# Attention, top-1 experts and a gated network in one program: V copied on chip, a third q/k buffer, decay rows on another queue, expert unit 0 inside attention's last steps

## The chip, the cores and the metric

The program runs on one NeuronCore of one Trainium2 chip. The metric is the device time of one execution in microseconds; the kernel before has a median of 932.3 us over three runs (931.89 to 935.76).

## The reference

Three stages follow each other, all in float32 as the caller sees it.

```python
# 1. causal attention with a decay, batch 4, 8 heads, 576 positions, head size 64
scores = q @ k.T / 8 + cum[:, None] - cum[None, :]      # cum: running sum of log f
attn   = softmax(where(causal, scores, -1e9));  x = attn @ v
# 2. top-1 mixture of 8 experts over the 2304 tokens (x: 512 wide)
logits = x @ w_gate + modality_bias[modality_id];  e = argmax(logits)
x      = gate_w * (relu(x @ w1[e]) @ w2[e])             # w1: 512x1024, w2: 1024x512
# 3. gated network
out    = (sigmoid(x @ w_gate2) * (x @ w_val)) @ w_out   # 512 -> 1536 -> 512
```

## The kernel before

Attention works on 16 pairs: one head of two batches at a time (the second batch in reversed order, so that both halves fill the array). `Attention.run` is a software pipeline over n. In one step it takes the scores and exponentials of pair n, the transposes of q and k of pair n+1 (`prep`) and its decay mask (`mask`), the transposed probabilities and the product with V of pair n-1 (`probs`, `values`), and the division by the sums and the gate logits of pair n-2 (`normalise`, `logits`). The order of these pieces inside a step is written out by hand in `Attention.ORDER`: QA to QD are score products, T the additions of the mask with the running maximum, E the exponentials, PQ, PK, PR with pq, pk, prq, prk the transposes of q and k and their copies, X, Y, Z, W with their small letters the probabilities, A, AH, M the products with V, N1, N0, N2 the normalisation, D the mask, LQ, LV, LD the loads, L one piece of later work. Each engine receives its instructions in that order (manual schedule) and runs them in order.

Loads are issued by SyncE: q and k into raw buffers (`load_qk`), V into buffers `vr` (`load_v`) and two decay rows per pair, spread over all lanes (`load_dec`). The mask of pair 0 is made on VectorE, the others on GpSimd. V's pieces are loaded in two layouts, so some rows are read twice from memory.

When the first half of the tokens is done, small routing pieces (`Routing.early`) are taken from a list: they choose the first two blocks of tokens, units 0 and 1, while attention goes on, and fetch their rows. `Experts` splits each weight piece into a high and a low part for products of full precision. Unit 0's pieces are loaded and split by `begin`, after attention, into spare buffers of attention (decay masks and scores); its eight blocks of products (`pair`: up, relu, down) stand in the order behind attention. `Routing.finish` is the rest of the routing, a long chain on VectorE; its result is needed from unit 2 on, and unit 1 follows it in the order.

Of the kernel before, what the change touches and what calls it, by code (L numbers as in the profile page):

```python
# [84 lines left out]
class Attention:  # L85


    NV, NR = 3, 2
    ORDER = (
        "QA ot QB om PK T1 Y0 pk W w ra LQ Ta Z y0 X0 z Tb x0 LV N1 PQ T0 n1 E1 X1 x1 QC pq E4 QD PR prq T3 "  # L90
        "prk Y1 E3 N2 A0 D y1 M N0 AH E0 T2 n2 rc A3 A2 E2 LD A1 L L"
    )

    def __init__(self, tc, ctx, top, ro, ps, q, k, v, f):
# [11 lines left out]
        self.spares = 0  # L106
# [9 lines left out]
        nc.sync.dma_start(fs, f.rearrange("b h s -> (b h) s"))  # L116
        self.load_qk(0)
        V = nc.vector
# [7 lines left out]
        nc.sync.dma_start(self.drow[0], cum)  # L126
        nc.sync.dma_start(
# [10 lines left out]
    def spare(self, tag, shape, dt):  # L138

        if tag == "s":  # L140
            self.spares += 1
            pool, tag = ((self.ps_, "sc"), (self.pd, "dec"))[(self.spares - 1) // 2 % 2 == 0]
        else:
            pool, tag = {"e": (self.pe, "raw"), "t": (self.pt, "qk")}[tag]
        return pool.tile(shape, dt, tag=tag, name="e" + tag)
# [19 lines left out]
    def load_v(self, n):  # L165
# [241 lines left out]
    def run(self):  # L407
# [3 lines left out]
        while n < N + 2 or late:  # L411
            step = {"L": lambda: late.pop(0)() if late else None}
            if n == 2:
                self.ro.biases()
            if n == 4:
                self.ro.tables()
            if 0 <= n + 1 < N:
                step |= {"LV": lambda: self.load_v(n + 1), "D": lambda: self.mask(n + 1)}
                step |= self.prep(n + 1)
            if n + 2 < N:  # L420
                step |= {"LQ": lambda: n + 2 and self.load_qk(n + 2), "LD": lambda: self.load_dec(n + 2)}
            if 0 <= n < N:
                step |= self.scores(n)
# [8 lines left out]
            for key in self.ORDER.split():  # L432
                if key in step:
                    step[key]()
            if n == 0:
                self.ro.load()
            if 2 <= n < N + 2 and n % 2:
                late += self.ro.columns(*self.pairs[n - 2])
            n += 1


class Routing:
# [43 lines left out]
    def load(self):  # L486
# [1150 lines left out]
```

## Time and profile before

| | us |
|---|---|
| median of three runs | 932.3 |
| profiled execution, whole | 931.75 |
| its span, first to last instruction | 929.7 |
| TensorE busy | 874.8 (94%) |
| VectorE busy | 687.7 (74%) |
| ScalarE busy | 530.3 (57%) |
| GpSimd busy | 219.3 (24%) |

By stage, attention takes from the start to about 235 us, unit 0 lies from 232 to 257, the other units end near 484, and the gated network fills the rest. An engine that is off the path may stand idle without cost; the rows below therefore show stretches and single waits, not only sums. In a timeline the bracket at a row's end is the idle time of that engine before the row, and what ended it.

### The profile page before, as it was taken

Reading aid. Unit: us, or ns where it says so; the run is one execution under the profiler, and the core shown is the slowest. Engines: PE = TensorE matmul, PEld = TensorE weight load, DVE = VectorE, ACT = ScalarE, POOL = GpSimd, SP = SyncE. Lnnn points to the kernel's source line nnn. Section 1 sums busy time; section 2 is a strip of 40 time slices with the busy share of each in tenths; the row PEclk is TensorE's granted clock in tenths of the full one; section 3 lists DMA queues with packets and bytes.
Section 4 is the critical chain, followed back from the end, with each engine's and each line's share of the span. In section 5 each row is a group of like instructions: output and inputs, shape, how many; then the busy total and the mean of one; then the engine's idle time right before and its main releaser. Section 6 shows DMA issues by size and latency. Waiting matters only on the chain. (4 is left out here: it accounts for less than half of the span.)

```text
span 929.7 us, 16504 instructions
## 1 busy us (share of the span) xinstructions
PE 874.8 (94%) x5535; PEld 763.3 (82%) x5535; DVE 687.7 (74%) x1676; ACT 530.3 (57%) x1139; POOL 219.3 (24%) x457
## 2 busy tenths in 40 slices
PE   5899999868989999999989989999999999999996
PEld 3677667646879999999879878899998999999995
DVE  6567668864878999999856786988656888666662
ACT  3467667634356666666855455556545556544442
POOL 2678767486032222211000000001100001100002
PEclk8799999988999999999999999999999999999998
DMA  6577867985573695558928442225312222322201
GB/s 149 107 169 161 128 148 183 127 216 123 115 255 117 217 322 186 172 179 268 308 74 296 128 139 95 72 69 169 104 65 68 68 69 87 118 69 68 68 1 68
DMA packets 128411, 128.87 MB, mean 139 GB/s; under 512 B 75264, under 2 KB 102400, under 8 KB 128320
## 3 DMA queue, kind: packets, MB, share of 16 engines
q1 hardware_dynamic: 123680, 113.05, 44.3%
q0 software_dynamic: 4640, 14.70, 4.6%
q8 instruction: 45, 0.74, 0.3%
q14 instruction: 46, 0.38, 0.1%
HBM read 129.13 MB, written 24.28 MB: 165 GB/s over the span
## 5 line engine op out<-in xcount | busy, mean ns | idle before, releaser
L1335 PE MATMUL g<-x,wc 128*128 128x384 f32 x1536 | 303.4, 339 | 9.6 <-ACT pc L1372 3.1
L1335 PEld LDWEIGHTS g<-x,wc 128*128 128x128 f32 x1536 | 275.0, 189 | 29.9 <-ACT pc L1372 4.4
L1423 PE MATMUL o<-wo,ah 128*128 128x512 f32 x648 | 184.5, 397 | 0.2 <-DVE ah L1360 0.2
L1423 PEld LDWEIGHTS o<-wo,ah 128*128 128x128 f32 x648 | 118.0, 188 | 11.6 <-DVE ah L1360 1.0
L1431 POOL DMA_INDIRECT out_dram<-os,tok x18 | 18.4, 1021 | 421.7 <-ACT os L1430 416.2
L934 DVE TENSOR_TENSOR wl<-ws,wh 128x1024 fp32r<-128x1024 f32 x80 | 97.1, 1216 | 0.0
L928 ACT ACTIVATE wh<-ws 128x1024 fp32r<-128x1024 f32 x80 | 84.6, 1059 | 18.6 <-PE y L1010 18.6
L1359 ACT ACTIVATE ah<-s 128x384 fp32r<-128x384 f32 x72 | 37.9, 526 | 99.5 <-DVE s L1358 96.1
L272 ACT ACTIVATE sc<-sc,mn 128x192 f32<-128x192 f32 (+2 forms) x144 | 82.4, 577 | 7.2 <-DVE mn L264 7.1
L197 POOL TENSOR_SCALAR dec<-cum 128x192 f32<-128x192 f32 (+4 forms) x150 | 78.8, 533 | 18.6 <-DMA cum<-drow 15.5
L264 DVE CUSTOM_DVE_ANT_0 sc<-s,dec 128x192 f32<-128x192 f32 (+2 forms) x144 | 58.8, 441 | 23.4 <-PE s L257 18.3
L1000 PE MATMUL h<-xh,wh 128*128 128x256 f32 x256 | 74.2, 290 | 0.0
L1000 PE MATMUL h<-xh,wl 128*128 128x256 f32 x256 | 73.0, 285 | 0.7 <-DVE wl L934 0.7
L1000 PE MATMUL h<-xl,wh 128*128 128x256 f32 x256 | 73.0, 285 | 0.6 <-DVE xl L955 0.6
L980 POOL DMA_INDIRECT rows_by_expert<-ys,dst x20 | 22.8, 1138 | 197.5 <-ACT hh L970 135.0
L1372 ACT ACTIVATE pc<-g 128x384 f32<-128x384 f32 x96 | 46.3, 482 | 31.1 <-PE g L1335 31.1
L1218 DVE TENSOR_TENSOR wc<-wf,wc 128x512 fp32r<-128x512 f32 x72 | 40.7, 568 | 29.1 <-ACT wc L1215 29.1
L257 PE MATMUL s<-qk,qT 64*128 64x320 f32 (+4 forms) x384 | 60.0, 439 | 1.4 <-ACT qT L221 0.7
L291 PE MATMUL t<-ident,sc 128*128 128x128 f32 x320 | 50.5, 293 | 9.2 <-ACT py L297 6.7
L257 PEld LDWEIGHTS s<-qk,qT 64*128 64x128 f32 (+1 forms) x384 | 33.8, 192 | 27.6 <-issue 20.1
L1000 PEld LDWEIGHTS h<-xl,wh 128*128 128x128 f32 x256 | 49.4, 193 | 2.3 <-DVE xl L955 0.8
L1351 ACT ACTIVATE sg<-sg 128x384 f32<-128x384 f32 x48 | 25.2, 525 | 45.3 <-DVE sg L1381 18.8
(281 smaller groups left out, 1765.1 us busy)
## 6 DMA issues: line engine op xcount, KB each, us to landing
ws<-in_moe_w_dram SPq DMA_DIRECT2D x80, 512.0 KB
wf<-wd SPq DMA_DIRECT2D x36, 512.0 KB
cum<-drow SPq DMA_DIRECT2D x32, 288.0 KB
wd<-dec SPq DMA_DIRECT2D x18, 512.0 KB
wof<-wd SPq DMA_DIRECT2D x18, 512.0 KB
raw<-in_moe_w_gate_dram SPq DMA_DIRECT2D x12, 512.0 KB
raw<-in_moe_w_val_dram SPq DMA_DIRECT2D x12, 512.0 KB
raw<-in_moe_w_out_dram SPq DMA_DIRECT2D x12, 512.0 KB
```

The lines of the kernel that those rows point to most:

```text
L197: (nc.gpsimd if n else nc.vector).tensor_scalar(d[r, o], c[r, z], -1.0, c[r, a:a + 1], ALU.mult, ALU.add)
L257: nc.tensor.matmul(out[r, o:o + w], q[a, rows], k[a, c:c + w], start=True, stop=True)
L264: nc.vector.tensor_tensor_reduce(s[:, so + c0:so + e], t[j, b, c0][:, 0:e - c0], d[:, do + c0:do + e], -1.0, mn[j][:, 5:6] if c0 else 3.0e ...
L272: nc.scalar.activation(so, so, AF.Exp, bias=mn[j][:, b:b + 1], scale=-1.0, accum_out=sm[:, c:c + 1])
L291: nc.tensor.transpose(dst, s[:, o:o + P], self.ident)
L928: self.nc.scalar.activation(hi, self.wraw(u, k), AF.Copy)
L934: ins = eng.tensor_tensor(lo, self.wraw(u, k), hi.bitcast(F32), ALU.subtract)
L1000: nc.tensor.matmul(t, a[:, c, cs], b[:, c, :], start=(n == 0), stop=(n == 3 * KD - 1))
L1218: V(t["w"][:, 1, to], of(), t["w"][:, 0, to].bitcast(F32), ALU.subtract)
L1335: self.nc.tensor.matmul(t, p[:, c, :], q[:, c, :], start=(first and n == 0), stop=(n == total - 1), skip_group_check=not first)
L1372: nc.scalar.activation(c, t, AF.Copy)
L1423: nc.tensor.matmul(o[0], x[:, cs], y[:, r, :], start=(o[1] == 0 and k == 0), stop=(o[1] == 2 * self.NP - 1 and k == 2))
```

## The change

The table `ORDER` is written anew, and a table `TAIL` is added for the two steps that only drain (steps 16 and 17). The number of V buffers goes from 3 to 2 and that of the raw q/k buffers from 2 to 3. q and k are loaded for pair n+3 in step n; V is loaded for pair n, at the head of step n. Of V the repeated chunks are not loaded again but copied on ScalarE (`copy_v`, VC in the table). f, the running sums and the first pair's decay rows are issued by ScalarE. The gate logits begin with a copy, and the modality bias is added at head 3.

Unit 0 is prepared inside attention: its rows are fetched in step 13, its first four weight pieces are loaded at the end of step 13 and the other four at the end of step 15, its x is transposed in step 14, and its blocks (U in the table) stand between the pieces of steps 16 and 17. Pieces 0 and 1 are split on GpSimd, 2 and 3 (P2, P3) on ScalarE and VectorE, the others as before. The conversion of the four destination indices moves from ScalarE to GpSimd.

```diff
-    NV, NR = 3, 2
+    NV, NR = 2, 3
...
+    TAIL = (
+        "om ot U N1 n1 P2 U N2 N0 n2 Y0 y0 X0 x0 Z z X1 x1 Y1 y1 ra W w P3 U A0 M A1 A2 AH A3 rc U",
+        "U ot om U N1 n1 N2 N0 n2 U",
+    )
...
-        nc.sync.dma_start(fs, f.rearrange("b h s -> (b h) s"))
+        nc.scalar.dma_start(fs, f.rearrange("b h s -> (b h) s"))
         self.load_qk(0)
+        self.load_qk(1)
...
-        nc.sync.dma_start(self.drow[0], cum)
-        nc.sync.dma_start(
+        nc.scalar.dma_start(self.drow[0], cum)
+        nc.scalar.dma_start(
...
-        nc.sync.dma_start(t[0:64, 0, 4:9], a[:, 0:9:2])
+        nc.sync.dma_start(t[0:64, 0, 8], a[:, 8])
+        nc.sync.dma_start(t[64:P, 1, 8], b[:, 8])
         nc.sync.dma_start(t[0:64, 1, 4], b[:, 0])
-        nc.sync.dma_start(t[64:P, 1, 5:9], b[:, 2:9:2])
+
+    def copy_v(self, n):
+
+        t = self.vr[n % self.NV]
+        self.nc.scalar.activation(t[0:64, 0, 4:8], t[0:64, 0, 0:4], AF.Copy)
+        self.nc.scalar.activation(t[64:P, 1, 5:8], t[64:P, 1, 1:4], AF.Copy)
...
-            nc.sync.dma_start(t, self.drow[j, r:r + 1, :].to_broadcast([P, S]))
+            (nc.sync if n else nc.scalar).dma_start(t, self.drow[j, r:r + 1, :].to_broadcast([P, S]))
...
+            if 2 <= n + 3 < N:
+                step["LQ"] = lambda: self.load_qk(n + 3)
             if 0 <= n < N:
+                step |= {"LV": lambda: self.load_v(n), "VC": lambda: self.copy_v(n)}
...
-        nc.gpsimd.tensor_tensor(self.lg[:, sl], t[:, 0:k], (self.lg if h else self.bt)[:, sl], ALU.add)
+        lg, t = self.lg[:, sl], t[:, 0:k]
+        if h == 0:
+            nc.gpsimd.tensor_copy(lg, t)
+        else:
+            nc.gpsimd.tensor_tensor(lg, t, lg, ALU.add)
+        if h == 3:
+            nc.gpsimd.tensor_tensor(lg, lg, self.bt[:, sl], ALU.add)
...
-            nc.scalar.activation(self.dst0, dst, AF.Copy)
+            g.tensor_copy(self.dst0, dst)
...
-    POOL0 = 0, 1, 2, 3
+    POOL0 = 0, 1
...
-    def begin(self, att):
+    def prepare0(self, att, part):
 
         self.att = att
-        for k in range(8):
-            self.raw[k] = att.spare("e", [P, 1024], F32)
-        for k in range(8):
+        if part == 0:
+            for k in range(8):
+                self.raw[k] = att.spare("e", [P, 1024], F32)
+        for k in range(4 * part, 4 * part + 4):
             self.load(0, k)
-        for p in range(4):
-            self.high(0, p)
-            self.low(0, p)
-        self.run0 = self.pair(0, self.step0)
-        for f in range(8):
+        if part:
+            for p in self.POOL0:
+                self.split0(p)
+            self.run0, self.n0 = self.pair(0, self.step0), 0
+
+    def split0(self, p):
+        self.high(0, p)
+        self.low(0, p)
+
+    def advance(self):
+        if self.n0 < 8:
+            self.n0 += 1
             next(self.run0)
+
+    def begin(self):
+        while self.n0 < 8:
+            self.advance()
...
-        ro.then = [lambda c=c: ex.transpose(0, c) for c in range(0, KD, 2)]
+        none = lambda: None
+        ro.then = [lambda: ex.prepare0(att, 0)] + [lambda c=c: ex.transpose(0, c) for c in range(0, KD, 2)]
+        ro.then += [none, none, lambda: ex.prepare0(att, 1)]
```

Line numbers shift: a score product is L257 before and L263 now, a unit's up-projection L1000 and L1039, its down-projection L1010 and L1049.

VectorE at the start, before: the copies of k (`qk<-t`), the mask of pair 0 (`dec<-cum`) and the first addition (`sc,mn<-s,dec`).

```order
L125 SCALAR_TENSOR_TENSOR x<-ones,x 32x576
L484 COPY iw<-ident 64x8x64 x2
L219 COPY qk<-t 128x512
L219 COPY qk<-t 128x64
L197 TENSOR_SCALAR dec<-cum 128x192 x2
L197 TENSOR_SCALAR dec<-cum 128x576 x2
L197 TENSOR_SCALAR dec<-cum 64x64 x2
L197 TENSOR_SCALAR dec<-cum 128x448 x2
L197 TENSOR_SCALAR dec<-cum 128x320 x2
L264 ISA sc,mn<-s,dec 128x192
```

The same place now:

```order
L129 SCALAR_TENSOR_TENSOR x<-ones,x 32x576
L501 COPY iw<-ident 64x8x64 x2
L225 COPY qk<-t 128x64
L203 TENSOR_SCALAR dec<-cum 128x192 x2
L203 TENSOR_SCALAR dec<-cum 128x576 x2
L203 TENSOR_SCALAR dec<-cum 64x64 x2
L203 TENSOR_SCALAR dec<-cum 128x448 x2
L203 TENSOR_SCALAR dec<-cum 128x320 x2
L225 COPY qk<-t 128x512
L270 ISA sc,mn<-s,dec 128x192
```

The large copy of k has moved from ahead of the mask to behind it.

GpSimd in step 15, before: splits of unit 0's pieces (`edec<-eraw`), the logits of the normalisation (`lg<-lt`), the destination indices (`dstf`) and the fetch of the rows (`xg`).

```order
L926 TENSOR_SCALAR edec<-eraw 128x1024
L558 TENSOR_TENSOR lg<-lt,lg 128x24
L693 TENSOR_SCALAR pad_3339<-slot,n_90 128x2
L934 TENSOR_TENSOR edec<-eraw,edec 128x1024
L696 TENSOR_TENSOR dstf<-pad_3339,slot 128x2
L693 TENSOR_SCALAR pad_3339<-slot,n_90 128x2
L695 TENSOR_SCALAR row_3340<-slot,n_90 128x2
L696 TENSOR_TENSOR dstf<-pad_3339,row_3340 128x2
L697 TENSOR_TENSOR nt<-n_90 128x1
L702 DMA xg_92<-xd,ids_75 128x513
```

GpSimd from step 15 to step 17 now (the split buffers are all named `spare`):

```order
L581 TENSOR_TENSOR lg<-lt,lg 128x48
L338 TENSOR_SCALAR r<-sm 128x9
L581 TENSOR_TENSOR lg<-lt,lg 128x24
L965 TENSOR_SCALAR spare<-spare 128x1024
L973 TENSOR_TENSOR spare<-spare 128x1024
L965 TENSOR_SCALAR spare<-spare 128x1024
L973 TENSOR_TENSOR spare<-spare 128x1024
L581 TENSOR_TENSOR lg<-lt,lg 128x48
L581 TENSOR_TENSOR lg<-lt,lg 128x24
L338 TENSOR_SCALAR r<-sm 128x9
```

The fetch and the indices have left this place for steps 13 and 14; the splits of pieces 0 and 1 stand behind the logits of step 15, ahead of those of step 16.

TensorE at the end of step 15, before: the products with V of pair 14 (`o<-py,vr`), unit 0's transposes (`x<-ident,xg`), then the probabilities of pair 15 (`t<-ident,sc`).

```order
L348 MATMUL o<-py_3358,vr_126 64x384
L348 MATMUL o<-py_3359,vr_126 64x384
L953 MATMUL x<-ident,xg_92 128x128 x2
L953 MATMUL x<-ident,xg_93 128x128 x2
L953 MATMUL x<-ident,xg_92 128x128 x2
L953 MATMUL x<-ident,xg_93 128x128 x2
L291 MATMUL t<-ident,sc 128x128 x4
```

TensorE at the end of step 15 now: unit 0's first block (`h<-xh,spare`) follows the products with V at once, and the normalisation (`t<-iw,ot`) comes behind it.

```order
L354 MATMUL o<-py_3431,vr_124 64x128
L354 MATMUL o<-py_3432,vr_124 64x128
L1039 MATMUL h<-xh_3394,spare 128x256
L1039 MATMUL h<-xl_3395,spare 128x256
L1039 MATMUL h<-xh_3394,spare 128x256 x2
L1039 MATMUL h<-xl_3395,spare 128x256
L1039 MATMUL h<-xh_3394,spare 128x256 x2
L1039 MATMUL h<-xl_3395,spare 128x256
L1039 MATMUL h<-xh_3394,spare 128x256 x2
L1039 MATMUL h<-xl_3395,spare 128x256
L1039 MATMUL h<-xh_3394,spare 128x256
L395 MATMUL t<-iw,ot 128x144 x3
```

Unit 0's eight blocks stood behind the last product with V; now seven of them lie between there and the last normalisation, and the eighth follows it.

## Rows read from the trace of the kernel before

**Rows 1.** Table of stretches: length, busy time (instructions), granted clock, DMA share, GB/s.

```profile
66.00:112.00 46.00, 46.00 (x436) 33.94 (x434) 32.96 (x132) 32.13 (x97) 36.38 (x113) 1.00 0.81 154
...
42.00:44.00 2.00, 2.00 (x11) 2.00 (x10) 0.69 (x1) 0.51 (x1) 0.00 (x0) 0.50 0.41 94
```

**Rows 2.** Timeline of TensorE, one undisturbed step: start, us, line, operation.

```profile
53.96 1.83 PE L257 MATMUL s<-qk,qT 64*128 64x256 f32 x16
55.72 0.66 PE L226 MATMUL t<-ident,kr 128*128 128x128 f32 x4
56.21 0.60 PE L291 MATMUL t<-ident,sc 128*128 128x128 f32 x4
...
58.09 0.92 PE L389 MATMUL t<-iw,ot 128*128 128x144 f32 x6
58.85 0.60 PE L226 MATMUL t<-ident,qr 128*128 128x128 f32 x4
...
62.36 1.08 PE L348 MATMUL o<-px,vr 128*64 128x512 f32 x4
...
65.37 1.83 PE L257 MATMUL s<-qk,qT 64*128 64x256 f32 x16
```

**Rows 3.** Timeline of TensorE at the head and in the transition.

```profile
10.31 3.24 PE L257 MATMUL s<-qk,qT 64*128 64x256 f32 x16 [0.38 <-ACT qT L221]
...
41.46 1.09 PE L226 MATMUL t<-ident,kr 128*128 128x128 f32 x4 [3.10 <-DMA kr<-in_k_dram]
...
198.89 1.83 PE L257 MATMUL s<-qk,qT 64*128 64x256 f32 x16
...
209.04 1.12 PE L291 MATMUL t<-ident,sc 128*128 128x128 f32 x4 [6.75 <-ACT py L297]
```

**Rows 4.** Waits of TensorE, 60 to 200 us: total, times, longest.

```profile
PE t L226 <- DMA kr<-in_k_dram: 5.9, 4, 3.1
```

**Rows 5.** Timeline of TensorE: a down and an up of unit 0; unit 1's start.

```profile
240.47 1.52 PE L1010 MATMUL y<-edec,eqk 128*128 128x512 f32 x6
241.83 0.28 PE L1000 MATMUL h<-xh,esc 128*128 128x256 f32 x1
...
260.51 0.39 PE L1000 MATMUL h<-xh,wl 128*128 128x256 f32 x1 [0.75 <-DVE wl L934]
```

**Rows 6.** Timelines of GpSimd and ScalarE in step 15.

```profile
202.49 1.04 POOL L926 TENSOR_SCALAR edec<-eraw 128x1024 fp32r<-128x1024 f32 x1
...
204.22 2.34 POOL L934 TENSOR_TENSOR edec<-eraw,edec 128x1024 fp32r<-128x1024 f32 x1
...
207.81 0.20 ACT L698 ACTIVATE dst<-dstf 128x4 int32<-128x4 f32 x1 [8.63 <-POOL dstf L696]
```

**Rows 7.** Timeline of VectorE at the start.

```profile
8.69 0.69 DVE L219 COPY qk<-t 128x512 f32<-128x512 f32 x1 [1.98 <-PE t L226]
...
12.66 3.21 DVE L197 TENSOR_SCALAR dec<-cum 128x192 f32<-128x192 f32 x9 [0.70 <-DMA cum<-drow]
...
15.79 0.34 DVE L264 CUSTOM_DVE_ANT_0 sc<-s,dec 128x192 f32<-128x192 f32 x1
```

**Rows 8.** Timelines of SyncE and TensorE at the start.

```profile
4.92 0.62 SPq L163 DMA_DIRECT2D kr<-in_k_dram  x1
...
7.57 1.09 PE L226 MATMUL t<-ident,kr 128*128 128x128 f32 x4 [7.57 <-DMA kr<-in_k_dram]
```

**Rows 9.** Groups: line, operation, shapes, count; busy us, mean ns; idle before.

```profile
L970 ACT ACTIVATE hh<-h 128x256 fp32r<-128x256 f32 x64 | 24.7, 386 | 37.9 <-PE h L1000 36.4 <-DVE wl L934 0.6
...
L971 DVE SCALAR_TENSOR_TENSOR eqk<-h,eqk 128x256 fp32r<-128x256 f32 x8 | 3.2, 412 | 0.2 <-ACT eqk L970 0.2
...
L934 DVE TENSOR_TENSOR edec<-eraw,edec 128x1024 fp32r<-128x1024 f32 x2 | 2.4, 1216 | 0.0
```

**Rows 10.** Timeline of VectorE: first and last piece of the routing's chain.

```profile
235.59 0.23 DVE L583 TENSOR_REDUCE lm<-lg 128x9 f32<-128x72 f32 x1 [0.35 <-POOL lg L558]
...
255.55 1.35 DVE L631 TENSOR_TENSOR bm<-dg,lane 128x1152 bf16<-128x1152 f32 x1
```

More of the change, by code (lines that the diff above doesn't have):

```diff
@@ L138, in spare @@
     def spare(self, tag, shape, dt):
[L140 to L145, printed above, removed]
+        pool, tag = {"e": (self.pe, "raw"), "t": (self.pt, "qk"), 0: (self.pd, "dec"), 1: (self.ps_, "sc")}[tag]
+        return pool.tile(shape, dt, tag=tag, name="spare")
     def bank(self, shape=(P, 512)):
@@ L405, in normalise, with run, one @@
         return two("N1 n1", part(1, 3, 0)) | two("N2 N0 n2", part(4, 1, 1))
-    def run(self):
+    def run(self, ex):
         N = len(self.pairs)
         late, outs, n = [], {}, -2
[L411 to L414, printed above, removed]
+        def one():
+            if late:
+                late.pop(0)()
+        while n < N + 2:
+            step = dict.fromkeys(("L1", "L2", "L3"), one)
             if n == 4:
                 self.ro.tables()
+                self.ro.biases()
             if 0 <= n + 1 < N:
-                step |= {"LV": lambda: self.load_v(n + 1), "D": lambda: self.mask(n + 1)}
+                step["D"] = lambda: self.mask(n + 1)
                 step |= self.prep(n + 1)
             if n + 2 < N:
-                step |= {"LQ": lambda: n + 2 and self.load_qk(n + 2), "LD": lambda: self.load_dec(n + 2)}
+                step["LD"] = lambda: self.load_dec(n + 2)
+            if 2 <= n + 3 < N:
+                step["LQ"] = lambda: self.load_qk(n + 3)
             if 0 <= n < N:
+                step |= {"LV": lambda: self.load_v(n), "VC": lambda: self.copy_v(n)}
                 step |= self.scores(n)
@@ L431, in run @@
                 step |= self.sums(n - 1) | now
-            for key in self.ORDER.split():
+            step |= {"U": ex.advance, "P2": lambda: ex.split0(2), "P3": lambda: ex.split0(3)}
+            for key in (self.ORDER if n < N else self.TAIL[n - N]).split():
                 if key in step:
@@ L435, in run @@
             if n == 0:
+                self.ro.load_w()
+            if n == 2:
                 self.ro.load()
             if 2 <= n < N + 2 and n % 2:
-                late += self.ro.columns(*self.pairs[n - 2])
+                new = self.ro.columns(*self.pairs[n - 2])
+                late = new + late if len(new) == 1 else late + new
             n += 1
+        assert not late
 class Routing:
@@ L689, in ids, with places @@
             st["collect"](self.ps_t.tile([P, 2, 2 * NE], F32, tag="t", name="t", bufs=TB))
+        def places():
             pad, row, dst, g = t("pad0", [P, 2]), t("row0", [P, 2]), t("dstf", [P, 2 * NE]), nc.gpsimd
@@ L705, in fetch @@
                 )
-        return [count] + [lambda i=i: choose(i) for i in range(NE)] + [slots, lambda: None, ids, fetch] + self.then
+        return [count] + [lambda i=i: choose(i) for i in range(NE)] + [slots, lambda: None, ids, fetch, places] + self.then
     def finish(self, tmp, ps):
@@ L917, in part @@
             if kind == "h":
-                self.two = self.att.spare("s", [P, 2, 1024], F32R)
+                self.two = self.att.spare(p % 2, [P, 2, 1024], F32R)
             return self.two[:, "hl".index(kind)]
```

16 lines of the change are left out of this document (8 added, 8 removed).

## Prediction

> **What bounds the kernel now.** I read, in this order, the table of stretches, TensorE's timeline, the list of waits, and the timelines of the other engines where TensorE stands still. Throughout, "step n" is one pass of the attention loop: scores of pair n, preparation of pair n+1, values of pair n-1, normalisation of pair n-2. Pair 15 is the last, so steps 16 and 17 only drain.
>
> From 66 to 112 us TensorE is busy for the whole 46 us, while VectorE is busy 32.96, ScalarE 32.13 and GpSimd 36.38 [rows 1]. There the array sets the pace, and a step from one first score product to the next takes 65.37 - 53.96 = 11.41 us [rows 2]. For one step that makes 8.2 us on VectorE, 8.0 on ScalarE and 9.0 on GpSimd, so each has at least 2.4 us to spare. No reordering makes such a step shorter. What can be won are the places where TensorE stands still or runs at half its clock, and there are three.
>
> Head: the first scores stand at 10.31 and those of step 3 at 53.96 [rows 2, 3]. The sixteen score products at 10.31 take 3.24 us, the same at 53.96 only 1.83: half the clock. At 41.46 TensorE has waited 3.10 us for k [rows 3], and from 42 to 44 the granted clock is 0.50, 1.2 instead of 2.4 GHz [rows 1].
>
> Steps 3 to 14: 198.89 - 53.96 = 144.9 us for twelve steps, where 12 x 11.41 = 136.9 would do: 8.0 lost. The list of waits gives k 5.9 of them [rows 2 to 4]; 2.1 have other causes.
>
> Transition: from the last first score product (198.89) to the point where expert unit 1 has its first low half (260.51) pass 61.6 us [rows 3, 5]. In them stand 6.75 us before 209.04 [rows 3]. The cause is on ScalarE: a copy of four numbers waits 8.63 us for GpSimd, which is splitting weights (1.04 and 2.34 us a piece), and the eviction that TensorE needs is queued behind it [rows 6].
>
> **The change, part by part.** The sum is made against the profiled execution's own 931.75 us (span 929.7 and 2.05 around it); the median of the three runs is 932.3.
>
> *Head.* The first decay rows leave SyncE's queue, but on VectorE pair 0's mask now stands ahead of the copy of k that the first scores need. Before, the mask's nine later pieces began at 12.66 and ended at 15.87, where the first addition starts (15.79) [rows 7]. Now the copy (0.69) follows at 15.9, the scores start at 16.6, and at half clock the first of them are through some 1.6 us later: first addition at 18.2, 2.4 us late. The next copy of k also moved behind most of step 0's additions, so that step 1 starts near 26: from 16.6 twice 3.24 for the two cold sets of scores, 1.09 for k's transposes, 0.69 for its copy, 1.1 for gaps. What comes back: step 1 has no normalisation (0.76 and about 0.4), so 10.2 us, and some 2.5 for half clock; step 2 then runs 11.41 without the wait of 3.10 and its half clock. So 26 + 12.7 + 11.4 = 50.1, and I add 0.8 for gaps: 50.9 instead of 53.96, **3.0 won**. Ends: 3 lost (the mask later, step 1 cold throughout) to 8 won.
>
> The row shows the second pair of decay rows in VectorE's hands at 12.66, when only one queue was issuing [rows 7]. The Trainium skill, "DMA: Bandwidth & Descriptors", section "Issuing engines are not separate DMA queues", says that transfers from either queue interleave on the same 16 engines and that only issue time is saved. The first q/k load was in use at 7.57 [rows 8]; by that rule a second one right behind it would be in by about 14, an estimate, and the decay rows that share the engines with it would come up to 1.3 us later, so that the sum would be 12.6 instead of 13.9. I charge nothing for it, because no row here has two such queues active.
>
> *Steps 3 to 14.* With a third pair of raw buffers q/k are asked for three pairs ahead, a step earlier in relation to their use. V's two repeated pieces shrink from five and four chunks of 64 rows to one each (9 to 2), so 448 of some 3,970 packets a step go. The k waits (5.9) therefore fall away; TensorE's own pace is next. The two copies that fill the halves again are shown by no row; the nearest is a ScalarE activation of 128x256 at 386 ns [rows 9], which is an upper end for 64 lanes x 256 and 192, with nothing as the lower. I take 0.75 a step: 8.0 + 0.75 stays under 11.41, so they cost nothing in themselves. They stand between the last exponential and the eviction of the output. If that eviction came late, the normalisation on TensorE would wait, 2.9 us into the next step; this is a rival below. The logits' first write becomes a copy, and the bias is added at head 3: a short GpSimd operation per half and pair, in its 2.4 us of room. The four gathers and the eight transposes of unit 0 (2 x 0.49) now run in steps 13 and 14. So 136.9 + 2.1 (kept) + 1.0 = 140.0 against 144.9: **4.9 won**. Ends: 1 (other waits replace half of those) to 7.5.
>
> *Transition.* I lay it out from the last step's first score product as zero. The step without preparation (ten transposes, four of which take 0.49) takes 10.2 us [rows 2]. The copy of four numbers is now GpSimd's own, so nothing on ScalarE waits for GpSimd, and the 6.75 us go. Late next: unit 0's first block needs weight piece 0, whose split stands on GpSimd behind the last normalisation's logits (about 9.9): 9.9 + 1.04 + 2.34 = 13.3, so TensorE waits about 3.1. Then one up-projection of 1.4 (241.83 - 240.47 is the six down products, 1.36, and a pair is about 2.77) [rows 5]: 14.7. Normalisation 0.8: 15.5. Second block 2.8, normalisation 0.5, 25 transposes at 0.122 with 0.5 for their banks 3.5: 22.3. Third block 2.8, values 2.9, three blocks 8.3, last normalisation 0.7: 37.0. VectorE and GpSimd need 1.5 more before the routing's first reduction: 38.5.
>
> Now the part that speaks against the change. The routing's chain on VectorE ran from 235.59 to the end of the second one-hot table (255.55 + 1.35), 21.3 us [rows 10], while TensorE was working off unit 0. In it stood four of unit 0's low halves (1.22) and eight relu remainders (0.41) [rows 9]; now two remainders are left: 21.3 - 4.9 - 3.3 + 0.8 = 13.9, so 52.4. Only then come unit 1's low halves of x and of the first weight piece, with two more routing operations between, 2.9: 55.3. TensorE has spent unit 0 by 44 and stands idle for 10 us behind VectorE's chain. Unit 0 in the gaps wins the gaps, and loses the cover of that chain. 61.6 - 55.3 = 6.3; I take 0.3 off for the ranks' products and their semaphores: **6.0 won**. Ends: the wait of 3.1 may bring half clock (the wait at 41.46 did), which by that stretch is some 2.9 us, and other waits may add 3: nothing won; at best 9, if piece 0 is ready in time.
>
> Sum: 3.0 + 4.9 + 6.0 = 13.9. 931.75 - 13.9 = 917.9, called **918**. The experts from unit 1 on and the gated network have the same instructions and are left as they are.
>
> **The rivals.**
> *A, more is won.* The decay rows land with the first q/k and the head's cold stretch shrinks: first addition at 15.8 (2.4), step 1 at full clock (2.5), piece 0 split in time (3.1): 8 more, 910. For it: GpSimd has room, and the new order starts pair 1's mask earlier. Against it: the mask still stands ahead of the copy of k.
> *B, the chain's cover is missed.* Each microsecond by which the last normalisation is late passes to the end, since nothing on TensorE hides VectorE's chain any longer. With half clock in step 16 (2.9) and evictions late by 3, the transition wins nothing: 931.75 - 7.9 = 924. For it: this stretch lost its clock before. Against it: ScalarE and VectorE are less full there than in a normal step.
> *C, k is late for want of bandwidth, not of lead.* Then 5.9 and 3.1 of the waits stay: 13.9 - 9.0 = 4.9, 927. For it: 4 MB of weights now fall into the last steps. Against it: twelve steps lost 5.9 us to k in four places only, not in each.
> *D, slower.* V has two buffers instead of three, so its load starts only when the values of two pairs ago are done, at the step's start, and ScalarE must have it at that step's end for the copies. ScalarE works in order: if V is late, the output's eviction and then TensorE's normalisation wait. SyncE issues six pieces at about 0.6 us each, 3.8 us, and the first k of all was in use at 7.57, 2.0 us after the end of its last issue (4.92 + 0.62) [rows 8]: with twice that for fuller queues V is there 6 to 8 us into a step, and the copies come near 10.5. It decides from 1 us of lateness a step (15 x 1 against 13.9); with V landing at 12.5, 2 us a step or 30 in all, the time would be 948.
>
> **How the numbers follow.** Forecast 0.54 (its own range 912 to 923), A 0.17, B 0.14, C 0.08, D 0.07. The range reaches beyond A for a head and a transition both at their better ends (8 + 7.5 + 9 = 24.5 would be 907) and to C with a little more: 905 to 929. Within 0.5% of 932.3 is 927.6 to 937.0, about what a measurement of this kernel can tell from no change. Faster: forecast, A, B and a part of C, 0.86; same: the rest of C and a mild D, 0.08; slower: D, 0.06.
>
> **What would show it.** Right: no wait of TensorE for k after the head; steps of 11.4 to 11.7 us; step 3's scores near 51 and step 15's near 191; no wait on ScalarE for GpSimd; an idle TensorE of 8 to 11 us between unit 0 and unit 1, ended by VectorE; a first addition later than 15.79. Wrong: steps over 12 us with ScalarE waiting for V (D); k waits as before (C); an idle stretch over 13 us or a last normalisation later than 40 us after the last step's start (B); step 3 before 47 (A). It would also be wrong if the stages after unit 1's start moved by more than 2 us.

## The result, and the profile after

The changed kernel takes 937.3 us (median of 18 runs, 932.7 to 946.1) against 932.3 (18 runs) beside it: ratio 1.0054, 95% interval 1.0034 to 1.0074. The forecast was 918 us, range 905 to 929: wrong, and on the other side. In a second set of 12 runs the ratio was 1.0031 (1.0013 to 1.0050). One of the 18 runs of the kernel before took 2175.9 us; it does not move the median.

The first profile came from the longest of the 18 runs (946.08 us whole, span 944.3). A second one, of a run of 937.0 us (span 935.2), shows the same waits and is used for the sums; in the first, the stretch from step 15's scores to unit 1's first low half is 3.9 us longer. A span is cut by four marks: the first scores of step 3, those of step 15, the first reduction of the routing on VectorE behind the last normalisation, and unit 1's first low half on TensorE. For the kernel before they stand at 53.96, 198.89, 235.59 and 260.51 [rows 2, 3, 5, 10].

| | step 3 at | steps 3 to 15 | to the reduction | to unit 1's low half | to the span's end |
|---|---|---|---|---|---|
| before | 54.0 | 144.9 | 36.7 | 24.9 | 669.2 |
| forecast | 50.9 | 140.0 | 38.5 | 17.1 | 669.2 |
| after, 1st profile | 51.9 | 153.4 | 47.0 | 22.2 | 669.8 |
| after, 2nd profile | 49.8 | 151.9 | 43.8 | 21.5 | 668.3 |

So the head won about what was forecast (2.1 and 4.2 us instead of 3.0), the experts and the gated network are the same, and two stages are longer than forecast by 12 and 10 us (second profile), and longer than before by 7 and 4.

Timeline of TensorE after, second profile (start, us, line, operation): first scores of steps 3, 12, 13 and 15, and the waits of step 12 between them.

```profile
49.78 1.83 PE L263 MATMUL s<-qk,qT 64*128 64x256 f32 x16
...
156.62 1.83 PE L263 MATMUL s<-qk,qT 64*128 64x256 f32 x16
...
163.27 1.81 PE L395 MATMUL t<-iw,ot 128*128 128x144 f32 x6 [2.85 <-DVE qk L225]
...
168.40 0.63 PE L232 MATMUL t<-ident,qr 128*128 128x128 f32 x4 [1.73 <-issue]
...
177.22 1.83 PE L263 MATMUL s<-qk,qT 64*128 64x256 f32 x16
...
201.65 1.83 PE L263 MATMUL s<-qk,qT 64*128 64x256 f32 x16
```

An undisturbed step takes 11.52 us here (11.41 before, [rows 2]). Step 12 takes 20.6, step 8 13.0, step 14 12.8, step 10 12.6 and step 11 12.1; these five hold 14.1 of the 15.0 us above 12 x 11.41. No wait for k is left after the head ([rows 4]: 5.9 us before). In its place stand the 2.85 in step 12 and 1.24 in step 8, behind VectorE's copy of k, which waits for ScalarE's copy of q. ScalarE's timeline tells what that waited for:

```profile
109.00 0.42 ACT L180 ACTIVATE vr<-vr 64x256 f32<-64x256 f32 x1 [1.97 <-DMA vr<-in_v_dram]
...
161.42 0.42 ACT L180 ACTIVATE vr<-vr 64x256 f32<-64x256 f32 x1 [5.16 <-DMA vr<-in_v_dram]
```

V is late for its copies in two steps by 2 and 5 us, and in all the others by 0.4 or nothing: rival D's mechanism, but not in every step. What these two share is told by the waits of SyncE's queue, 60 to 180 us (total, times, longest):

```profile
SPq L160 <- DMA xd<-x: 4.7, 1, 4.7
SPq L190 <- DMA xd<-x: 3.7, 1, 3.7
...
SPq L163 <- DMA xd<-x: 3.0, 1, 3.0
SPq L174 <- DMA xd<-x: 2.5, 1, 2.5
```

xd is where the finished token rows go, some 1.2 MB at a time, four times in the kernel. V's load stands behind such a write each time, and SyncE itself is held up in issuing the loads that follow the write.

The transition shows the same write. Timeline of SyncE after, second profile: the last write, and the first of twelve loads for unit 1.

```profile
247.10 0.37 SPq L595 DMA_DIRECT2D xd<-x  x1
...
249.91 22.30 SPq L941 DMA_DIRECT2D ws<-in_moe_w_dram  x12
```

ScalarE's timeline of the same: the first weight split, and what it waited for.

```profile
263.01 1.06 ACT L967 ACTIVATE wh<-ws 128x1024 fp32r<-128x1024 f32 x1 [13.68 <-DMA ws<-in_moe_w_dram]
```

TensorE's timeline of the same, from step 17 to unit 1's first low half:

```profile
238.72 0.55 PE L1039 MATMUL h<-xh,spare 128*128 128x256 f32 x1 [2.63 <-DVE ot L381]
...
242.86 1.14 PE L395 MATMUL t<-iw,ot 128*128 128x144 f32 x8
...
258.97 0.56 PE L668 MATMUL t<-am,bm 128*128 128x54 bf16 x9 [6.50 <-DVE am L662]
...
264.61 0.58 PE L1039 MATMUL h<-xh,wh 128*128 128x256 f32 x1 [3.78 <-ACT xh L993]
...
266.95 0.58 PE L1039 MATMUL h<-xh,wl 128*128 128x256 f32 x1 [1.03 <-DVE wl L973]
```

Unit 1's first weights are asked for at 249.91, right behind the last write, and ScalarE has them at 263.01, 13.1 us later. TensorE has done all of unit 0 by 252.5 and then does little for 12 us: 6.50 us for VectorE's one-hot tables, 3.78 for x, which ScalarE has to split behind the weight. The table of stretches (length, busy time of TensorE, its weight loads, VectorE, ScalarE and GpSimd, granted clock, DMA share, GB/s) shows the write from its start to its end, and the loads behind it:

```profile
248.00:250.00 2.00, 2.00 (x14) 1.79 (x13) 1.92 (x12) 0.38 (x1) 0.00 (x0) 1.00 1.01 285
...
252.00:254.00 2.00, 0.47 (x5) 0.23 (x3) 2.00 (x16) 0.00 (x0) 0.00 (x0) 1.00 1.16 84
254.00:256.00 2.00, 0.00 (x0) 0.00 (x0) 2.00 (x11) 0.00 (x0) 0.00 (x0) 0.79 1.13 87
256.00:258.00 2.00, 0.00 (x0) 0.00 (x0) 2.00 (x4) 0.00 (x0) 0.00 (x0) 0.50 1.13 116
...
262.00:264.00 2.00, 0.00 (x0) 0.00 (x0) 0.00 (x0) 0.99 (x2) 0.00 (x0) 0.50 1.07 384
```

The write starts at 285 GB/s and then falls to 84; from there on the DMA engines are as full during the write as during the loads, at 84 to 116 GB/s instead of 384. And TensorE, idle, has fallen to 0.50 of its clock (1.2 GHz).

### The profile page after: what moved, and what is told of

The parts are those of the page before. It is cut to its first block, busy times and chain, and to the rows that moved or that the text cites. A ratio compares the mean times of both kernels' runs of the same rounds, so it can differ in the third digit from the quotient of the medians.

```text
span 944.3 us, 16565 instructions
## 1 busy us (share of the span) xinstructions
PE 877.6 (93%) x5535; PEld 762.1 (81%) x5535; DVE 688.1 (73%) x1677; ACT 547.8 (58%) x1172; POOL 212.4 (22%) x458
## 5 line engine op out<-in xcount | busy, mean ns | idle before, releaser
L1470 POOL DMA_INDIRECT out_dram<-os,tok x18 | 18.4, 1021 | 421.8 <-ACT os L1469 416.3
L1039 PE MATMUL h<-xh,wh 128*128 128x256 f32 x256 | 74.8, 292 | 4.5 <-ACT xh L993 4.5
L1039 PE MATMUL h<-xh,wl 128*128 128x256 f32 x256 | 73.7, 288 | 1.0 <-DVE wl L973 1.0
L1039 PE MATMUL h<-xl,wh 128*128 128x256 f32 x256 | 73.6, 288 | 0.1
L263 PE MATMUL s<-qk,qT 64*128 64x320 f32 (+4 forms) x384 | 57.7, 424 | 12.1 <-DVE qk L225 11.2
L263 PEld LDWEIGHTS s<-qk,qT 64*128 64x128 f32 (+1 forms) x384 | 32.4, 185 | 32.7 <-issue 28.5
L1039 PEld LDWEIGHTS h<-xh,wh 128*128 128x128 f32 x256 | 50.0, 195 | 6.2 <-ACT xh L993 4.6
L1039 PEld LDWEIGHTS h<-xl,wh 128*128 128x128 f32 x256 | 49.9, 195 | 1.9 <-DVE xl L994 0.4
```

The costliest lines, as they stand in the source:

```text
L263: nc.tensor.matmul(out[r, o:o + w], q[a, rows], k[a, c:c + w], start=True, stop=True)
L1039: nc.tensor.matmul(t, a[:, c, cs], b[:, c, :], start=(n == 0), stop=(n == 3 * KD - 1))
```

## The experiments

Each ran beside the kernel before on one chip, in four sets on four chips; ratios are to that kernel, with 95% intervals. The theories: **S**, the writes make V late, and ScalarE in order holds up the rest; **R**, routing work on VectorE in the middle of a step does it; **C**, unit 0 had covered the chain behind the last normalisation, so putting it ahead starts that chain later; **G**, the gaps are worth the filling, and the loss is half clock and waits.

Six of these profiles are of code that is the same up to step 15: the two of the changed kernel, u0_behind, u0_half, u0_two_blocks and weights_first. They show how far single lengths differ without any edit: step 8 takes 13.0 to 17.1 us, step 12 17.6 to 21.3, and steps 3 to 15 149.9 to 155.0. The kernel before and before_dst0_pool, alike up to there too, take 144.9 and 149.5. A length inside these bounds shows no gain; a named wait that is gone still says something.

**after_again.** The changed kernel unchanged.

> The changed kernel as it is, beside the variants on one chip. All theories expect 1.004 to 1.007 times the kernel before; the profile shows whether the waits of steps 8 and 12 (V 2.3 and 4.8 us late) and the 69 us from step 15's first scores to unit 1's first low half are its ordinary course or belonged to one slow run (then they are smaller by 5 us or more).

1.0031 (1.0013 to 1.0050). The waits and the long step 12 are its ordinary course; this is the second profile above.

### Steps 3 to 15

**v_three.** V in three buffers, loaded a step ahead (q two, k three raw buffers, for room).

```diff
-                step |= {"LV": lambda: self.load_v(n), "VC": lambda: self.copy_v(n)}
+                step["VC"] = lambda: self.copy_v(n)
...
-                step["D"] = lambda: self.mask(n + 1)
+                step |= {"LV": lambda: self.load_v(n + 1), "D": lambda: self.mask(n + 1)}
```

> The changed kernel with V in three buffers and loaded one step ahead, as in the kernel before (q keeps two raw buffers and k three, to make room); the halves are still copied on ScalarE. Theory S (V is late behind the write of the token rows, and ScalarE, working in order, holds up the rest): ScalarE's waits for V (2.3 and 4.8 us) vanish, step 8 comes back from 13.5 to about 11.6 us and step 12 from 20.7 to about 13, the time falls by 6 to 9 us to 929 to 931. Rival R (the routing's table work on VectorE in step 12 and the clock make the loss, V is only beside it): step 12 stays over 16 us and the time within 2 us of the changed kernel, 935 to 938.

1.0029 (1.0007 to 1.0051): no gain beyond 2 us, steps 3 to 15 take 156.3 us. ScalarE no longer waits for V anywhere, and yet step 12 takes 18.5 us, inside the bounds above, and step 10 takes 16.7: theory S alone falls. With q back at two buffers a wait for k of 1.14 us returns, so this version also gives something away. VectorE's timeline there, the last of the routing's tables and the next addition:

```profile
166.18 1.36 DVE L656 TENSOR_TENSOR bm<-dg,lane 128x1152 bf16<-128x1152 f32 x1
167.47 0.41 DVE L270 CUSTOM_DVE_ANT_0 sc<-s,dec 128x256 f32<-128x256 f32 x1
```

TensorE's timeline there:

```profile
168.92 1.08 PE L232 MATMUL t<-ident,qr 128*128 128x128 f32 x4 [2.94 <-issue]
```

That is also the first row at half clock there (1.08 instead of 0.63). The routing's tables run on VectorE from 163.65 to 167.5, and the additions of the same step stand behind them, so TensorE waits. The suspect is a key of the order that the prediction passed over: late pieces (the routing's, taken one by one from a list) now have a third slot, L3, which stands at a step's front, ahead of the additions Ta and Tb; before, both slots stood at its end.

**slot_end.** That slot at the step's end.

```diff
-        "QA LV T1 QB PR ot prq om X0 x0 prk LD L3 Y0 N1 Ta Z y0 n1 Tb X1 z T0 PQ ra Y1 x1 QC QD y1 pq E1 W N2 "
-        "T3 w LQ PK A0 E4 D N0 E0 pk M E3 T2 rc A1 A2 E2 n2 L2 VC AH A3 L1"
+        "QA LV T1 QB PR ot prq om X0 x0 prk LD Y0 N1 Ta Z y0 n1 Tb X1 z T0 PQ ra Y1 x1 QC QD y1 pq E1 W N2 "
+        "T3 w LQ PK A0 E4 D N0 E0 pk M E3 T2 rc A1 A2 E2 n2 L2 VC AH A3 L1 L3"
```

> The changed kernel with the third slot for late work moved from the step's front (ahead of the step's additions) to its end. Theory L (routing pieces in that slot hold up VectorE's additions, so TensorE waits for banks and loses its clock): step 10 is 11.6 us, and in step 12 the wait with no releaser (1.6 us) goes; but the writes of the token rows now stand directly ahead of V in SyncE's queue, so V is 4 to 5 us late twice: in all 0 to 4 us better than the changed kernel. Theory S alone (V behind the writes is everything): step 8 gets worse as step 12 is now, 3 to 8 us slower than the changed kernel.

1.0066 (1.0041 to 1.0090), some 3 us more than the changed kernel beside it (1.0031; the intervals overlap), where theory L expected 0 to 4 us less. Steps 3 to 11 take 104.4 us, 11.6 each (106.8 in the changed kernel): step 10 is 11.52, as theory L (R with its place named) has it, and step 8 only 11.9, so a late V costs little there. So for step 10 the slot's place is shown to be the cause. But step 12 still takes 17.7 and step 14 15.6, and steps 3 to 15 with 150.8 lie inside the bounds above.

**slot_end_v_three.** Both.

> Both: the third slot at the step's end, and V in three buffers one step ahead. Theories L and S together: neither the late V nor the routing pieces stop TensorE; the twelve steps from 3 to 15 take 141 to 144 us instead of 153, the ratio to the kernel before falls to 0.993 to 0.996. Rival (bandwidth: the write takes the sixteen engines whatever the order, and q, k or the decay rows come late in V's place): two steps still lose 3 us or more each, ratio 1.000 or above.

1.0097 (1.0068 to 1.0126): missed, slower. Steps 3 to 11 take 104.3 us, so up to there both causes are out. Step 12 takes 19.0, for a new reason, and in step 14 (15.5) the gathered rows are late. TensorE's timeline:

```profile
172.94 0.38 PE L668 MATMUL t<-am,bm 128*128 128x8 bf16 x9 [5.66 <-POOL am L661]
...
200.84 1.30 PE L992 MATMUL x<-ident,xg 128*128 128x128 f32 x6 [2.29 <-DMA xg<-xd,ids]
```

GpSimd multiplies am at 172.64, behind the whole mask of the next pair. The list has one empty piece between the tables and the product that collects them; with two slots to a step that was a step of distance, with three slots at one place it is none. The mask is late as well: GpSimd has waited 1.92 and 0.52 us for its decay rows, so the rival's full DMA engines are not excluded.

**respaced.** The same, with a second empty piece there, the transposes of unit 0 two slots later, and one more slot in step 16. The main line:

```diff
-        return [count] + [lambda i=i: choose(i) for i in range(NE)] + [slots, lambda: None, ids, fetch, places] + self.then
+        return [count] + [lambda i=i: choose(i) for i in range(NE)] + [slots, lambda: None, lambda: None, ids, fetch, places] + self.then
```

> The changed kernel with V in three buffers, the third slot at the step's end, and one more empty slot between the routing's tables and the product that collects them, the gathers ahead of unit 0's transposes by two steps (unit 0 still interleaved). Theory P (the twelve steps lose because dependent routing pieces, now three to a step, stand too close to each other and ahead of the step's own work): steps 3 to 15 take 140 to 142 us instead of 151.9, the ratio falls from 1.004 to 0.991 to 0.994. Rival (the sixteen DMA engines are full there and something else comes late): two steps still lose 3 us or more, 0.998 or above.

1.0025 (1.0005 to 1.0046). Steps 3 to 15 take 144.6 us, 7.2 less than in the changed kernel, below all six profiles above, and as long as before; the forecast of 140 to 142 is missed by a step 13 of 15.8, where the same tables end on VectorE at 170.9 and TensorE waits 2.08 and loses its clock. But from step 15's scores to unit 1's low half pass 69.6 us instead of 65.3 (69.2 in the first profile), so up to 4 us are given back, and the ratio is that of the changed kernel.

**send_act_queue.** The writes issued by ScalarE instead of SyncE.

```diff
-                nc.sync.dma_start(to[j, D:S].rearrange("(c p) d -> p c d", p=P), x[:, t0 + j:t0 + 8:2, lo:hi])
-                nc.sync.dma_start(to[j, 0:D], x[D * j:D * (j + 1), t0 + 8, lo:hi])
+                nc.scalar.dma_start(to[j, D:S].rearrange("(c p) d -> p c d", p=P), x[:, t0 + j:t0 + 8:2, lo:hi])
+                nc.scalar.dma_start(to[j, 0:D], x[D * j:D * (j + 1), t0 + 8, lo:hi])
```

> The changed kernel with the four writes of the token rows issued by ScalarE instead of SyncE. Theory Q (the price is the order in SyncE's queue, which waits for the write: 5.1, 3.4 and 2.9 us in the profile): q, k, V and unit 1's weights no longer wait for it, step 8 is 11.6, step 12 about 13, unit 1's weights are there 4 us earlier, 925 to 930. Rival E (the price is the sixteen engines' own time, which both queues share): V and the weights land as late as now, ScalarE pays some 2 us of issuing for each write, 937 to 941.

1.0268 (1.0228 to 1.0309), far slower, and both theories had it too cheap. ScalarE's timeline:

```profile
91.00 0.73 ACTq L595 DMA_DIRECT2D xd<-x  x1
98.46 0.45 ACTq L596 DMA_DIRECT2D xd<-x  x1
99.02 0.60 ACT L303 ACTIVATE py<-t 128x512 f32<-128x512 f32 x1 [10.18 <-DMA cum<-drow]
...
165.41 0.60 ACT L378 ACTIVATE ot<-o 128x512 f32<-128x512 f32 x1 [8.46 <-DMA xd<-x]
```

Now ScalarE's own queue is held up in issuing the write, for 10.2 and 8.5 us at two of the four writes, with all its work behind: between 91.73 and 98.46 it issues nothing. The Trainium skill, "DMA: Bandwidth & Descriptors", section "Issuing engines are not separate DMA queues", says that issuing on several engines saves only the time of issuing, and that this is usually small. Here it was not: 10.2 and 8.5 us on ScalarE, up to 4.7 on SyncE.

### The transition

**u0_behind, u0_half, u0_two_blocks.** None, four and two blocks of unit 0 ahead of the last normalisation, instead of six. (In the changed kernel six stand ahead of it and the seventh and eighth behind it, not seven and one. In u0_behind half an up-projection, 0.8 us, still runs ahead of it.) The tables of the first:

```diff
-        "om ot U N1 n1 P2 U N2 N0 n2 Y0 y0 X0 x0 Z z X1 x1 Y1 y1 ra W w P3 U A0 M A1 A2 AH A3 rc U",
-        "U ot om U N1 n1 N2 N0 n2 U",
+        "om ot N1 n1 P2 N2 N0 n2 Y0 y0 X0 x0 Z z X1 x1 Y1 y1 ra W w P3 A0 M A1 A2 AH A3 rc",
+        "ot om N1 n1 N2 N0 n2",
```

> The changed kernel with all eight blocks of expert unit 0 behind attention again; the splits of its first weights stay where they are. Theory C (unit 0 had covered the routing chain, the last write of the token rows and the load of unit 1's weights; in the gaps of attention it covers nothing): the last normalisation stands some 33 us after step 15's first scores instead of 44, unit 1 has its first low half some 55 us after them instead of 69, and the time is 923 to 927. Rival G (the gaps of the last two steps are worth what the change expected, and the loss of the transition is half clock and new waits inside it): taking unit 0 out leaves the gaps open, 3 us at most are won, 934 to 940.

> The changed kernel with four blocks of unit 0 in step 16 and none in step 17, so that four (11 us) stay behind the last normalisation. Theory C: the gaps of step 16 are filled and four blocks cover most of the routing chain, the waits for step 17's output (2.6 us) and its half clock go; unit 1 has its first low half some 54 us after step 15's first scores, 922 to 926, the same as with all eight behind or up to 3 us better. Rival G: what is won is the wait and the half clock of step 17 alone, 931 to 934, and better than all eight behind by 3 us or more.

> The changed kernel with two blocks of unit 0 in step 16 and six behind attention. Theory C with a price for each block (the routing's first reduction came 24.1, 36.4 and 43.8 us after step 15's first scores with none, four and six blocks ahead of it, so 3.1 to 3.3 us a block; unit 1's first low half came 21.5 to 24.8 us behind that reduction in all three): the reduction stands 30 to 31 us after step 15's first scores, unit 1's first low half 53.5 to 55 (49.0 with none, 59.5 with four), ratio 0.989 to 0.992. Rival (a threshold: the first blocks fill real gaps and only the later ones cost): reduction at 25 to 27, ratio 0.983 to 0.986.

| blocks ahead | ratio | step 15's scores to the reduction | from there to unit 1's low half |
|---|---|---|---|
| 0 | 0.9851 (0.9822 to 0.9880) | 24.1 | 24.8 |
| 2 | 0.9923 (0.9894 to 0.9952) | 31.4 | 23.8 |
| 4 | 0.9942 (0.9923 to 0.9961) | 36.4 | 23.0 |
| 6 (after, 2nd) | 1.0031 (1.0013 to 1.0050) | 43.8 | 21.5 |

VectorE's timeline with none ahead, the first reduction (201.65 + 43.8 = 245.42 in the changed kernel, 206.53 + 24.1 here):

```profile
230.67 0.23 DVE L608 TENSOR_REDUCE lm<-lg 128x9 f32<-128x72 f32 x1 [0.60 <-POOL lg L581]
```

The same with two ahead (step 15's scores at 204.83):

```profile
236.27 0.23 DVE L608 TENSOR_REDUCE lm<-lg 128x9 f32<-128x72 f32 x1 [0.60 <-POOL lg L581]
```

The same with four ahead (step 15's scores at 204.69):

```profile
241.11 0.23 DVE L608 TENSOR_REDUCE lm<-lg 128x9 f32<-128x72 f32 x1 [0.42 <-POOL lg L581]
```

Theory C's mechanism holds, and it is nearer to a line than to a threshold: two blocks more put the reduction back by 7.3, 5.0 and 7.4 us, 3.3 a block ((43.8 - 24.1) / 6; its products alone are 2.8). Two other profiles with six ahead have it at 47.0 (the first profile) and 45.7 (weights_first), so the price is 3.3 to 3.8. What follows the reduction takes 21 to 25 us in all four. Of the expected times only u0_behind's came true (923.7): u0_half took 932.0 where C had 922 to 926, since C had its four blocks fill gaps at no cost, and u0_two_blocks lies just above all its ranges. Theory G falls: without any block in the gaps the stretch from step 15's scores to the reduction has hardly a gap to fill. The table of stretches of u0_behind:

```profile
206.00:231.00 25.00, 22.34 (x207) 16.67 (x206) 15.77 (x55) 14.13 (x34) 14.88 (x24) 1.00 0.50 105
231.00:255.50 24.50, 22.94 (x159) 19.98 (x157) 23.98 (x82) 10.91 (x19) 0.00 (x0) 1.00 0.68 153
```

TensorE is idle for 2.7 of 25 us before the reduction and for 1.6 of 24.5 behind it, at full clock.

**weights_first.** The changed kernel with the last write behind the first four loads of unit 1's weights.

```diff
         for k in range(8):
             self.load(1, k)
+            if k == 3:
+                self.ro.send()
...
         self.gates(1)
-        self.send()
```

> The changed kernel with the last write of the token rows issued behind the first four loads of unit 1's weights instead of ahead of all eight. Theory W (the write takes some 10 us of the DMA engines, and unit 1 starts when its weights are in behind it): ScalarE's wait for the weights (13.7 us) shrinks by 8 us or more, unit 1 has its first low half 3 to 4 us earlier, when VectorE's chain is through, ratio 0.999 to 1.001. Rival (VectorE's routing chain ends last anyway): less than 1 us, 1.003 to 1.006.

0.9986 (0.9970 to 1.0002), 4 to 6 us better than the changed kernel. ScalarE's wait for the weights is gone, and the reduction (247.03) to unit 1's low half takes 17.7 us instead of 21.5. As the reduction itself stands at 45.7 there, the whole transition is 63.3 us instead of 65.3. TensorE's row:

```profile
264.68 0.58 PE L1040 MATMUL h<-xh,wl 128*128 128x256 f32 x1 [1.03 <-DVE wl L974]
```

So of the stretch behind the reduction 3.9 us are weights behind the write, as theory W has it.

**before_dst0_pool.** The kernel before with the copy of four numbers on GpSimd alone.

```diff
-            nc.scalar.activation(self.dst0, dst, AF.Copy)
+            g.tensor_copy(self.dst0, dst)
```

> The kernel before with one part of the change alone: the copy of four numbers made by GpSimd instead of ScalarE. Theory A (the 6.75 us before 209 were ScalarE waiting in order for GpSimd): the wait goes and all behind it moves up, 0.992 to 0.994. Rival (something else is late right behind it, GpSimd's splits above all): 2 us or less are won, 0.998 to 1.000.

1.0007 (0.9991 to 1.0022): nothing. The 6.75 us of [rows 3] are gone and another wait stands in their place. TensorE's timeline:

```profile
222.38 0.66 PE L953 MATMUL x<-ident,xg 128*128 128x128 f32 x2 [9.21 <-DMA xg<-xd,ids]
```

Unit 0's gathered rows are not there, because GpSimd issues the gathers from 211.70, behind a weight split that began at 207.16 (the split of 204.22 in [rows 6] is that one in the kernel before). In the changed kernel they are issued in step 13. So the copy should pay only together with earlier gathers; that pair alone was not run.

### Both together

**slot_end_v_three_u0_behind, respaced_u0_behind, spaced_early_u0_behind.** The three versions for the steps, each with all of unit 0 behind attention; the last has the spacing of respaced, but unit 0's transposes in step 14 and its weights in step 15.

> All three: third slot at the step's end, V in three buffers, all of unit 0 behind attention. If the losses of the twelve steps and of the transition are separate they add: 0.985 (unit 0 behind alone) less 0.009 to 0.012, so 0.973 to 0.977 of the kernel before. Rival: unit 0 behind attention had already absorbed part of the steps' loss (its first weights and gathers come later than its start), 0.980 or above.

> The same with all of unit 0 behind attention. If P holds and adds to what unit 0 gives behind attention (0.985): 0.971 to 0.976. Rival: unit 0's weights and transposes, prepared later now, are late for it and cost 5 us or more: 0.980 or above.

> All of unit 0 behind attention, V in three buffers, third slot at the step's end, one more empty slot behind the routing's tables, but the transposes in step 14 and the first weights in step 15 as in the changed kernel. If the 7 us were given back by moving these into step 15 and the drain: steps 3 to 15 take 145 to 146 us, step 15's first scores to unit 1's first low half 49 to 51 (55.7 with them moved), ratio 0.976 to 0.980, below both kernels and all other versions. Rival (whatever is won in the steps is lost behind them, because something else, such as the gathered rows, sets when unit 0 and the drain can run): 54 us or more there, 0.984 or above.

| | ratio | steps 3 to 15 | step 15's scores to unit 1's low half |
|---|---|---|---|
| u0_behind | 0.9851 (0.9822 to 0.9880) | 155.0 | 49.0 |
| slot_end_v_three_u0_behind | 0.9918 (0.9888 to 0.9947) | 155.6 | 50.1 |
| respaced_u0_behind | 0.9852 (0.9829 to 0.9875) | 144.6 | 55.7 |
| spaced_early_u0_behind | 0.9829 (0.9796 to 0.9862) | 148.1 | 49.8 |

All three miss what their first theory expected; the first two fall where the rival put them. respaced_u0_behind's profile has 10.5 us less in the steps than that of u0_behind (the longest of the six) and 6.7 more behind them: the work put off comes due in the drain, and the ratio is the same. Moving it back (the last row) keeps the transition at 49.8 and loses 3.40 us in step 14, where the gathered rows are late. TensorE's timeline of that version:

```profile
197.11 1.00 PE L992 MATMUL x<-ident,xg 128*128 128x128 f32 x6 [3.40 <-DMA xg<-xd,ids]
...
247.81 0.38 PE L1039 MATMUL h<-xh,wl 128*128 128x256 f32 x1 [0.75 <-DVE wl L973]
```

It took 918.0 us against 934.1 and beats the kernel before and the changed one, but its interval overlaps that of u0_behind, which differs from the changed kernel in two lines of the table.

## Why the prediction was wrong

Against the second profile's own 937.0 us, the terms were off by: head -1.1 (49.8 instead of 50.9), steps +11.9 (151.9 instead of 140.0), transition +9.7 (65.3 instead of 55.6), the rest -1.0 and the time outside the span -0.3. That makes 19.2, the miss from 917.9 but for rounding.

**Head: the size is right, in part by luck.** The first scores come late (17.58 and 19.71 instead of the forecast 16.6, 10.31 before [rows 3]). The decay rows, which now come beside the second q/k load and for whose delay the prediction charged nothing, were late: they were asked for at 8.30 and 8.71 instead of 7.68, and the mask's nine later pieces begin at 13.64 and 15.77 instead of 12.66. How much of that is sharing the DMA engines was not tried. So step 1 starts 1.6 us later than forecast (2.3 in the first profile). But it begins at full clock, which the prediction gave only to rival A, and takes 10.7 us (12.1) instead of 12.7, and the 0.8 for gaps is not needed. VectorE's and TensorE's timelines, second profile:

```profile
13.64 3.20 DVE L203 TENSOR_SCALAR dec<-cum 128x192 f32<-128x192 f32 x9 [1.22 <-DMA cum<-drow]
...
17.58 3.34 PE L263 MATMUL s<-qk,qT 64*128 64x256 f32 x16 [9.01 <-DVE qk L225]
...
27.56 1.83 PE L263 MATMUL s<-qk,qT 64*128 64x256 f32 x16 [0.88 <-DVE qk L225]
```

**Steps 3 to 14: the step that failed is "TensorE's own pace is next".** It made 140.0 us, and 151.9 were measured. The k waits did fall away. But the prediction followed k and V and not the list of late pieces, whose slots the new order moves and makes three of two. A wait for a load was read as lead that was short, although the kernel before already spoke for rival C: the longest of its k waits in this stretch ([rows 4]: 3.1) ended at 175.55, behind a write that SyncE had issued from 158.44 on. Its table of stretches, DMA share and GB/s last:

```profile
168.00:170.00 2.00, 2.00 (x38) 1.50 (x36) 1.89 (x12) 1.92 (x8) 1.84 (x6) 1.00 1.40 98
170.00:172.00 2.00, 2.00 (x16) 1.01 (x12) 1.72 (x11) 0.60 (x1) 1.83 (x5) 1.00 1.25 60
172.00:174.00 2.00, 0.40 (x6) 0.19 (x4) 0.80 (x6) 0.00 (x0) 2.00 (x7) 1.00 1.07 147
```

Full engines and few bytes: what went ahead of k in the queue counted there, and not lead alone. That is a reading of these rows; the kernel before was not run with the write elsewhere. Shown: the routing's pieces ahead of the additions cost step 10 its 1.1 us, and step 12 stays long with V in time; V's lateness alone can be taken away without gain; with both away, steps 3 to 11 run at 11.6 us; with the pieces spaced too, 7.2 of the 11.9 come back. Not settled: how step 12's 9 us divide between V and the tables, since each experiment that took one away brought another wait; and why the write is slow.

**Transition: the terms that failed are the 38.5 us to the reduction and the 17.1 us behind it.** The reduction came at 43.8. With no block ahead it came at 24.1 (u0_behind), where the forecast's own terms without blocks make 20.1 (10.2 + 0.8 + 0.5 + 3.5 + 2.9 + 0.7 + 1.5). So 4.0 of the 5.3 us are the drain itself, which was priced too short, and 1.3 the blocks: 19.7 where the forecast had 18.4, 15.3 of products and the wait of 3.1. In the 19.7 stand the 2.63 us wait and half clock in step 17: rival B's mechanism, and the last normalisation stands 41.2 us after step 15's scores, later than B's 40. The chain behind the reduction took 21.5 instead of 17.1. That was an omission, not a size: the chain on VectorE went as forecast (17.7 with the weights in time), but the last write and unit 1's weights behind it had also lain beneath unit 0.

What the change lost by the interleaving is another sum. The prediction said that unit 0 ahead of the last normalisation "wins the gaps, and loses the cover of that chain", and set its 55.6 against the 61.6 of the kernel before, never against the same change without the interleaving. Its own terms had that price: 20.1, and 24.9 for the covered chain, make 45.0, 10.6 less than 55.6. Measured, the other parts alone bring the stretch to 49.0 (u0_behind) with 2.7 us of gaps left; the interleaving then adds 16.3. Which of the other parts (the index copy, the earlier gathers, fewer splits on GpSimd) closes the gaps was not tried apart.

**The 6.75 us** were a right reading of who waits for whom. Alone the edit is worth nothing, because the gathered rows are late next.

**Rival D** had the right mechanism at the wrong place: two steps behind the writes, not all; its 948 asked for 2 us in each. The measured 937.3 lies at the upper edge of the band that the prediction called no change (927.6 to 937.0). The chances of 0.08 and 0.06 for same and slower were too small above all because no rival had the interleaving itself as a loss.

## What to carry to other kernels

Before work is put into gaps, ask how large the gaps are once the other edits are in, and what starts behind the last piece that the work delays: a chain of 21 to 25 us, started more than 3 us later for each block, made the filling a loss. Compare with the same change without the filling, and not only with the kernel before. A table that orders an engine's work has to be read for all its keys, those with no name of their own above all: a third slot for late pieces at another place cost time that no load explains. And a load that is late now and then, rather than always, asks what transfer went ahead of it.

## What the hardware showed that was not expected

Writing the token rows starts at 285 GB/s (share 1.01, 248 to 250 us) and falls to 84 to 110 with the sixteen DMA engines full (share 1.13 to 1.16); loading weights fills them (1.07 to 1.09) at 364 to 384. Four such writes of some 1.2 MB take about 10 us each. While one runs, the queue that issued it stands still in issuing its last pieces and what comes next: up to 4.7 us on SyncE, 10.2 and 8.5 on ScalarE when that engine issued it. Whether the shape of the rows is why was not tried.
